# Products with the values in a fused attention, FFN and MoE kernel: another grouping of the query columns

## The chip, the cores and the metric

The kernel runs on one core of one Trainium2 chip. The metric is the device time of one execution, in microseconds (us). All arithmetic is in fp32 or in the fp32r form that the matrix engine takes (fp32 values split into a high and a low part).

## The reference

Three layers follow one another: a causal attention with a forget gate, a feed-forward layer, and a top-1 mixture of experts. The change lies in the attention, in its last line (`attn @ v`).

```python
batch, n_heads, seq, head_dim = (4, 8, 576, 64)
scores = scale * np.matmul(q, k.transpose(0, 1, 3, 2))
decay = cum[:, :, :, None] - cum[:, :, None, :]      # cum = cumsum(log f)
scores = np.where(causal, -1e9, scores + decay)
attn = softmax(scores)
out = np.matmul(attn, v)                             # x of the FFN: 2304 tokens x 512
...
x = _moe_ref(x)      # x @ w_in, an activation, @ w_out
y = _moe2_ref(x)     # 8 experts, each token goes to one
```

## The kernel before, in words

**Order of the work.** Nothing in the kernel is ordered by a scheduler of the compiler. A planner inside the kernel file (class `Order`) runs the program as coroutines against a table of assumed costs: each step is a `Use(engine, ns, function, priority)`, takes and gives buffers, and waits for events. Where several steps stand ready for an engine, the lower priority number goes first. The order that comes out is the static order of each engine's queue on the chip. So a changed cost or event in one coroutine can move instructions of others.

**Attention.** The 32 heads are worked off in 16 pairs; heads j = 0, 1 of a pair lie side by side. For pair i, `attention` (coroutines `unit`, `head`) takes five blocks of queries in the order c = 4, 3, 2, 1, 0 (`SEQ`): c = 0 to 3 are 128 queries each, against 128(c+1) keys, both heads; c = 4 is the last 64 queries of both heads together, against all 576 keys. Per block: scores on TensorE (L529, L534, tile `SR`, priority 0.8), decay and maximum on VectorE (L584), exponential on ScalarE (L589), scaling by the row sums on GpSimd (L600), then transposes on TensorE into one of two PSUM banks `T` (L612, L614, priority 0), and a copy out of `T` into SBUF by ScalarE (L634) or, for head 0 with c = 2 or 3, by VectorE (L632). The transposed weights of c = 0 to 3 go into one tile `pt` per head (four buffers, so two pairs), those of c = 4 into a tile `pu` (one buffer). `T_None` in the profile is the bank while it holds c = 4.

**Products with the values.** There are two bursts per pair, each with the two heads side by side on the two 64-column halves of the array:

- `weighted_last` (L707, tile `U`, in a `T` bank): last 64 queries, five key blocks, 64 columns each; it waits for c = 4 (`last_ok`); a VectorE copy (L713) brings it to columns 512 to 575 of `xT`.
- `weighted` (L654, tile `X`): the first 512 queries, four key blocks of 512, 384, 256 and 128 columns; it waits for all eight transposed blocks of c = 0 to 3 (`heads_ok`); a ScalarE copy (L661) brings it to columns 0 to 511 of `xT`. Priority 1.

```python
yield Use("PE", 2250, values, 1)     # weighted
yield Use("PE", 1100, burst, 1)      # weighted_last
yield Use("DVE", 230, lambda: nc.vector.tensor_copy(xT[:, 512:], X[:, :64]), 0)
```

Both are counted in `pv_ok`; then `xT` is written to memory (L672), and for the first four pairs `first_block` also splits its first 256 columns straight into the FFN's first input block `px0` (L689, L690).

**What runs beside it.** As soon as the first four pairs are done, the first half of the FFN (`half0`: L882 into `hp`, L1011 into `accp`, priority 6 and 6.5) fills TensorE wherever the attention has nothing ready. Its next input block (`px1` and so on) is loaded when the last one has been used up. Its weights `wa` are converted from 64-bit in 16 pieces over ScalarE, VectorE and GpSimd (L825 to L837) beside the attention. Until the first FFN block is there, `keep_warm` (L731) puts idle matmuls of the identity into gaps, priority 9, into the bank of `X`. After the attention the remaining FFN and MoE layers (L882, L1011, L1023 in other tiles) follow on TensorE.

Of the kernel before, what the change touches and what calls it, by code (L numbers as in the profile page):

```python
# [9 lines left out]
F32 = mybir.dt.float32  # L10
# [8 lines left out]
P = 128  # L19
# [171 lines left out]
def dve(n, fn, prio=5.0, fast=False):  # L191
    return Use("DVE", 144 + n * (0.6 if fast else 1.05), fn, prio)
# [31 lines left out]
def kernel(  # L224
# [14 lines left out]
    nc = tc.nc  # L239
# [73 lines left out]
    pt_ok = {(i, j): Event() for i in range(NP) for j in (0, 1, None)}  # L313
    s_done = [Event(5) for _ in range(NP)]
    read_ok = {(i, c): Event(2 if c < 4 else 1) for i in range(NP) for c in range(5)}
    heads_ok = [Event(8) for _ in range(NP)]
    last_ok = [Event() for _ in range(NP)]
    pv_ok = [Event(2) for _ in range(NP)]
    att_ok = Event(NP)
# [184 lines left out]


    def take_pt(i):
        for j in (1, None, 0):
            g = yield (pt4_b if j is None else pt_b, 1)
            if j is None:
                pt4[i] = (ap.tile([P, 5 * P], F32, tag="pu", name=f"pu{i}", bufs=1), g)  # L510
            else:
                pt[i, j] = (ap.tile([P, 13 * P], F32, tag="pt", name=f"pt{i}_{j}", bufs=4), g)
            done(pt_ok[i, j])

    def unit(i, c, started):
# [57 lines left out]
    def head(i, j, c, p, gp_, bank, st, summed, scaled, left):  # L573
# [24 lines left out]
        else:  # L598
            yield scaled
        yield pool1(w, lambda: nc.gpsimd.tensor_scalar(pw, pw, st[:, 6 + n:7 + n], 1.0, ALU.mult,  # L600
                                                       ALU.mult), 0)
        yield pt_ok[i, j]
        dst = pt4[i][0] if c == 4 else pt[i, j][0]
        for part in ((0, 1, 2, 3), (4,)) if c == 4 else (tuple(range(c + 1)),):
            gt = yield (t_b, 1)
            T = psa.tile([P, 512], F32, tag=f"T{gt[0]}", name=f"T{i}_{j}{c}{part[0]}", bufs=1)
            last = part == (4,)

            def turn():
# [8 lines left out]
            if c == 4:  # L618
                n = P * len(part)
                src, dh = (T[:64, :P], dst[:64, 512:]) if last else (T, dst[:, :512])  # L620
            else:
                n = w
                src = T[:, :w].rearrange("p (k q) -> p k q", q=P)
                if c < 2:
                    dh = dst[:, P * c:P * c + 384 * (c + 1)].rearrange(
                        "p (k q) -> p k q", q=384)[:, :, :P]
                else:
                    a0 = P * (c - 2)
                    dh = dst[:, a0:a0 + 384 * (c + 1)].rearrange(
                        "p (k q) -> p k q", q=384)[:, :, 256:]  # L630
            if j == 0 and c >= 2:
                yield dve(n, lambda: nc.vector.tensor_copy(dh, src), 0)  # L632
            else:
                yield act(n, lambda: nc.scalar.copy(dh, src), 0)  # L634
            give(t_b, gt)
        done(last_ok[i] if c == 4 else heads_ok[i])

    def weighted(i):

# [1 line left out]
        yield v_ok[i]  # L641
        gx = yield (xt_b, 1)
        xT = xts[i] = ap.tile([P, S], F32, tag="xT", name=f"xT{i}", bufs=2)
        go(weighted_last(i))
        vt, gr = vs[i]
        yield heads_ok[i]
        yield heads_ok[i]
        g = yield (x_b, 1)
        X = psa.tile([P, 512], F32, tag="X", name=f"X{i}")

        def values():
            for kb in range(4):
                for j in range(2):
                    nc.tensor.matmul(  # L654
                        X[D * j:D * j + D, P * kb:], vt[:, kb, j],
                        pt[i, j][0][:, 512 * kb:512 * kb + 512 - P * kb], start=(kb == 0),
                        stop=(kb == 3), skip_group_check=True)
        yield Use("PE", 2250, values, 1)
        for j in range(2):
            give(pt_b, pt.pop((i, j))[1])  # L660
        yield act(512, lambda: nc.scalar.copy(xT[:, :512], X), 0)  # L661
        give(x_b, g)
        done(pv_ok[i])
        yield pv_ok[i]
        give(rawv_b, gr)
        if i < NPAIR:
            go(first_block(i, xT))
# [24 lines left out]
        done(split_ok[i])  # L692
        done(half0.x_ok[0])

    def weighted_last(i):


        yield last_ok[i]
        gt = yield (t_b, 1)
        X = psa.tile([P, 512], F32, tag=f"T{gt[0]}", name=f"U{i}", bufs=1)  # L700
        t, vt = pt4[i][0], vs[i][0]

        def burst():
            for kb in range(5):
                kr = 64 if kb == 4 else P
                for j in range(2):
                    nc.tensor.matmul(X[D * j:D * j + D, :64], vt[:kr, kb, j],  # L707
                                     t[:kr, P * kb + 64 * j:P * kb + 64 * j + 64],
                                     start=(kb == 0), stop=(kb == 4))
        yield Use("PE", 1100, burst, 1)  # L710
        give(pt4_b, pt4.pop(i)[1])
        xT = xts.pop(i)
        yield Use("DVE", 230, lambda: nc.vector.tensor_copy(xT[:, 512:], X[:, :64]), 0)  # L713
        give(t_b, gt)
        done(pv_ok[i])

# [966 lines left out]
```

## Time and profile before

| | |
|---|---|
| median of 3 runs | 866.98 us (866.78 to 869.88) |
| profiled execution, its time | 867.16 us |
| its span in the trace | 865.6 us |
| TensorE busy (PE) | 844.3 us, 98% |
| VectorE (DVE), ScalarE (ACT), GpSimd (POOL) busy | 464.6, 362.7, 304.2 us |
| products with the values, L654 and L707 | 256 and 320 records on PE, from 24.9 to 312.1 us |
| starts of the sixteen main products (L654) | 34.5, 51.9, 66.1, 81.4, 100.7, 124.0, 140.3, 160.2, 179.3, 196.9, 216.8, 235.4, 256.2, 273.9, 293.0, 310.1 us |
| first FFN matmul (`hp`) | 88.3 us |

PE is the matrix engine, PEld its weight loads. An fp32 matmul of the attention's products stands in the trace as two records (two passes); busy time counts a moment once, however many records overlap. A line of the timeline has the start, the length, the engine, the source line and operation, the tiles, the shapes and the count of records merged, and in brackets how long the engine had been idle and what released it. The length of a merged line runs to the modelled end of its last matmul, so the distance from its start to the next line's start is what the work costs the engine.

### The profile page before, as it was taken

The numbers are of one execution on the slowest core, as the hardware profiler recorded it, in microseconds if no ns is written. First come the engines' busy times: TensorE is split into PE (matmuls) and PEld (weight loads), VectorE is DVE, ScalarE is ACT, GpSimd is POOL, SyncE is SP. The second block draws the span as 40 slices with busy tenths as digits, with TensorE's granted clock in tenths as the row PEclk, the third lists the DMA queues.
The fourth block names the chain that finished last, engine by engine and source line by source line (L and its number), as shares of the span: only waits on it lengthen the run. The fifth ranks groups of instructions, "written<-read, shape, count | busy, mean of one in ns | idle before, by whom it ended". The sixth has DMA issues, their size and how long they took to land.

```text
span 865.6 us, 15076 instructions
## 1 busy us (share of the span) xinstructions
PE 844.3 (98%) x5384; PEld 693.4 (80%) x5384; DVE 464.6 (54%) x1108; ACT 362.7 (42%) x841; POOL 304.2 (35%) x407
## 2 busy tenths in 40 slices
PE   9999998999999999999899999999999999999997
PEld 7665776887777799999888888888898888887685
DVE  7797977666545537777754344467652531212121
ACT  5677766565556644434533243323343121212110
POOL 3566876555544442444432122222210033000000
PEclk9999999999999999999999999999999999999999
DMA  7997666574324235233611133645432111541220
GB/s 145 174 188 180 164 164 154 123 141 119 95 67 122 73 123 110 79 120 98 207 62 49 61 130 112 211 142 183 148 124 85 49 49 49 211 154 50 98 74 25
DMA packets 154251, 101.96 MB, mean 118 GB/s; under 512 B 102802, under 2 KB 125842, under 8 KB 154176
## 3 DMA queue, kind: packets, MB, share of 16 engines
q1 hardware_dynamic: 151008, 96.22, 40.8%
q0 software_dynamic: 2832, 4.22, 1.8%
q8 instruction: 43, 0.70, 0.4%
q10 hardware_dynamic: 336, 0.56, 0.2%
q14 instruction: 32, 0.26, 0.1%
HBM read 76.86 MB, written 24.49 MB: 117 GB/s over the span
## 4 chain that ended last, share of the span: by engine, by line
PE 82%; DVE 9%; POOL 3%; ACT 2%; issue 2%; DMA 2%; SPq 0%; ACTq 0%; DVEq 0%; POOLq 0%
PE hm L882 12%; PE hr L882 12%; PE hp L882 8%; PE accp L1011 7%; PE accr L1011 6%; PE accBr L1011 6%; PE accm L1023 6%; PE accBm L1023 6%; PE SR L534 4%; PE T L614 4%; PE X L654 4%; PE gt L1197 1%; DVE wbx L830 1%; POOL wb L837 1%; PE U L707 1%
## 5 line engine op out<-in xcount | busy, mean ns | idle before, releaser
L904 POOL TENSOR_TENSOR glr<-gr,ghr 128x512 fp32r<-128x512 f32 x36 | 47.3, 1315 | 147.3 <-PE accBr L1011 90.8
L600 POOL TENSOR_SCALAR P<-P,st 128x512 f32<-128x512 f32 (+3 forms) x128 | 77.0, 615 | 38.4 <-DVE st L596 25.1
L882 PE MATMUL hr<-rx,wb 128*128 128x512 f32 (+1 forms) x384 | 89.5, 367 | 0.0
L882 PE MATMUL hm<-mx,wm 128*128 128x512 f32 (+1 forms) x336 | 87.0, 379 | 0.0
L1011 PE MATMUL accp<-ghp,wa 128*128 128x256 f32 x576 | 83.4, 287 | 2.1 <-DVE x_7b L1044 1.7
L589 ACT ACTIVATE P<-P,st 128x512 f32<-128x512 f32 (+3 forms) x128 | 71.4, 559 | 32.8 <-DVE st L584 31.8
L913 DVE SCALAR_TENSOR_TENSOR glm<-hm,ghm 128x512 fp32r<-128x512 f32 x36 | 24.8, 689 | 103.1 <-PE accBm L1023 68.4
L1011 PEld LDWEIGHTS accp<-ghp,wa 128*128 128x128 f32 x576 | 73.7, 190 | 5.4 <-issue 2.2
L912 ACT ACTIVATE ghm<-hm 128x512 fp32r<-128x512 f32 x36 | 21.6, 599 | 132.5 <-PE accBm L1023 120.7
L882 PEld LDWEIGHTS hr<-rx,wb 128*128 128x128 f32 x384 | 65.6, 188 | 13.0
L882 PEld LDWEIGHTS hm<-mx,wm 128*128 128x128 f32 x336 | 61.0, 188 | 14.9 <-issue 3.4
L904 POOL TENSOR_TENSOR glp<-gp,ghp 128x512 fp32r<-128x512 f32 x36 | 48.8, 1357 | 60.7 <-ACT ghp L903 54.2
L584 DVE CUSTOM_DVE_ANT_0 P<-SR,cm 128x512 f32<-128x512 f32 (+3 forms) x96 | 45.1, 485 | 24.8 <-PE SR L534 22.2
L614 PE MATMUL T<-ident,P 128*128 128x128 f32 x320 | 52.4, 278 | 3.5 <-POOL P L600 2.9
L894 ACT ACTIVATE tr<-hr,quarter 128x512 f32<-128x512 f32 x36 | 24.7, 687 | 61.3 <-DVE gr L899 44.4
L634 ACT COPY pt<-T 128x512 f32<-128x512 f32 (+2 forms) x96 | 35.3, 391 | 36.0 <-PE T L614 35.3
L898 DVE SCALAR_TENSOR_TENSOR gr<-tr 128x512 f32<-128x512 f32 x36 | 25.9, 719 | 42.1 <-POOL glr L904 40.5
L614 PEld LDWEIGHTS T<-ident,P 128*128 128x128 f32 x320 | 36.8, 141 | 14.5 <-POOL P L600 6.3
L534 PE MATMUL SR<-kt,qt 64*128 64x384 f32 (+3 forms) x224 | 44.9, 478 | 2.8 <-DVE st L584 2.5
L1011 PE MATMUL accr<-ghr,wb 128*128 128x512 f32 (+1 forms) x160 | 47.0, 375 | 0.0
L1011 PE MATMUL accp<-glp,wa 128*128 128x256 f32 x288 | 46.3, 283 | 0.4 <-POOL glp L904 0.4
L1011 PE MATMUL accBr<-ghr,wb 128*128 128x512 f32 (+1 forms) x160 | 46.5, 372 | 0.0
(355 smaller groups left out, 1871.8 us busy)
## 6 DMA issues: line engine op xcount, KB each, us to landing
cm<-rows SPq DMA_DIRECT2D x24, 256.0 KB, 4.4
rawq<-in_q_dram SPq DMA_DIRECT2D x64, 72.0 KB, 3.9
rawk<-in_k_dram SPq DMA_DIRECT2D x64, 72.0 KB, 3.3
xs<-xT SPq DMA_DIRECT2D x16, 288.0 KB, 2.1
x2n<-nat SPq DMA_DIRECT2D x18, 256.0 KB, 4.9
war<-in_moe_w_in_dram SPq DMA_DIRECT2D x8, 512.0 KB, 4.7
war<-in_moe_w_out_dram SPq DMA_DIRECT2D x8, 512.0 KB, 4.6
rawv<-in_v_dram SPq DMA_DIRECT2D x32, 128.0 KB, 2.7
```

What stands on the lines that cost most here:

```text
L534: nc.tensor.matmul(bank[:, j, :w], qt[p, P * c:P * c + P], kt[p, :w], start=True, stop=i >= NSUM)
L584: yield dve(w + 80, lambda: nc.vector.tensor_tensor_reduce(out=pv_, in0=so, in1=m, scale=-0.125, scalar=3e38, op0=ALU.add, op1=ALU.min, ac ...
L589: yield act(w, lambda: nc.scalar.activation(pw, pw, AF.Exp, bias=st[:, n:n + 1], scale=-1.0, accum_out=st[:, 2 + n:3 + n]), 1, 330)
L600: yield pool1(w, lambda: nc.gpsimd.tensor_scalar(pw, pw, st[:, 6 + n:7 + n], 1.0, ALU.mult, ALU.mult), 0)
L614: nc.tensor.transpose(T[:, P * n:P * n + P], p[:, P * kb:P * kb + P], ident)
L634: yield act(n, lambda: nc.scalar.copy(dh, src), 0)
L654: nc.tensor.matmul(X[D * j:D * j + D, P * kb:], vt[:, kb, j], pt[i, j][0][:, 512 * kb:512 * kb + 512 - P * kb], start=(kb == 0), stop=(kb ...
L882: nc.tensor.matmul(oo, a[:, c, cs], x[c], start=(ip == 0 and c == 0), stop=(ip == 2 and c == KC - 1))
L898: yield dve(n, lambda: nc.vector.scalar_tensor_tensor(g, t, 0.5, t, ALU.min, ALU.mult), 2)
L904: yield pool2(n, lambda: nc.gpsimd.tensor_tensor(gl, g, f32(gh), ALU.subtract), 1)
L1011: nc.tensor.matmul(acc[d][:, :w], b[:, fc, P * d:P * d + P], g, start=(fc == 0 and ip == 0 and (not narrow or d % 2 == 0)), stop=(fc == NF ...
L1023: nc.tensor.matmul(acc[a * (4 // na)], g[:, P * a:P * a + P], b[:, fc], start=(fc == 0 and ip == 0), stop=(fc == NF - 1 and ip == 2))
```

## The change

The 64 queries of c = 4 join the main product: their transposed weights are now copied into the two `pt` tiles, behind the 384 columns of c = 1 to 3 in each key block, so that the main product has 448, 448, 320, 192 columns for four key blocks of 128 keys and 64 for the last 64 keys (which stay in a small `pu`). The first 128 queries (c = 0) leave it and get a product of their own: one matmul per head over 128 columns, in a `T` bank (`weighted_first`, tile `U`). The main product now waits for c = 1 to 3 and c = 4, the small one for c = 0, which is the last block of a pair. The planner's costs go from 2250 and 1100 to 2700 and 260 ns.

```diff
-    heads_ok = [Event(8) for _ in range(NP)]
+    heads_ok = [Event(6) for _ in range(NP)]
+    early_ok = [Event(2) for _ in range(NP)]
...
     def take_pt(i):
-        for j in (1, None, 0):
+        for j in (0, 1, None):
             g = yield (pt4_b if j is None else pt_b, 1)
             if j is None:
-                pt4[i] = (ap.tile([P, 5 * P], F32, tag="pu", name=f"pu{i}", bufs=1), g)
+                pt4[i] = (ap.tile([P, P], F32, tag="pu", name=f"pu{i}", bufs=1), g)
             else:
-                pt[i, j] = (ap.tile([P, 13 * P], F32, tag="pt", name=f"pt{i}_{j}", bufs=4), g)
+                pt[i, j] = (ap.tile([P, 15 * P], F32, tag="pt", name=f"pt{i}_{j}", bufs=4), g)
...
-        yield pt_ok[i, j]
-        dst = pt4[i][0] if c == 4 else pt[i, j][0]
+        for n_ in (0, 1, None) if c == 4 else (j,):
+            yield pt_ok[i, n_]
+
+        def spread(h):
+            return pt[i, h][0][:, P:].rearrange("p (k q) -> p k q", q=448)
...
+            if last:
+                yield act(P, lambda: nc.scalar.copy(pt4[i][0][:64], T[:64, :P]), 0)
+            elif c == 4:
+                for h in range(2):
+                    yield act(256, lambda: nc.scalar.copy(
+                        spread(h)[:, :, 384:],
+                        T.rearrange("p (k j q) -> p j k q", k=4, j=2)[:, h]), 0)
...
-        done(last_ok[i] if c == 4 else heads_ok[i])
+        done(last_ok[i] if c == 4 else heads_ok[i] if c else early_ok[i])
...
-        go(weighted_last(i))
+        go(weighted_first(i))
         vt, gr = vs[i]
         yield heads_ok[i]
-        yield heads_ok[i]
+        yield last_ok[i]
...
-            for kb in range(4):
+            for kb, (p0, o0, n) in enumerate(
+                    ((128, 0, 448), (576, 0, 448), (1152, 128, 320), (1728, 256, 192),
+                     (0, 384, 64))):
                 for j in range(2):
...
+                    if kb < 4:
+                        m, vk = pt[i, j][0][:, p0:p0 + n], vt[:, kb, j]
+                    else:
+                        m, vk = pt4[i][0][:64, 64 * j:64 * j + 64], vt[:64, 4, j]
+                    nc.tensor.matmul(X[D * j:D * j + D, o0:o0 + n], vk, m, start=(kb == 0),
+                                     stop=(kb == 4), skip_group_check=True)
-        yield Use("PE", 2250, values, 1)
-        for j in range(2):
-            give(pt_b, pt.pop((i, j))[1])
-        yield act(512, lambda: nc.scalar.copy(xT[:, :512], X), 0)
+        yield Use("PE", 2700, values, 1)
+        give(pt4_b, pt4.pop(i)[1])
+        yield act(448, lambda: nc.scalar.copy(xT[:, P:], X[:, :448]), 0)
         give(x_b, g)
         done(pv_ok[i])
         yield pv_ok[i]
+        for j in range(2):
+            give(pt_b, pt.pop((i, j))[1])
...
-    def weighted_last(i):
+    def weighted_first(i):
-        yield last_ok[i]
+        yield early_ok[i]
...
-            for kb in range(5):
-                kr = 64 if kb == 4 else P
-                for j in range(2):
-                    nc.tensor.matmul(X[D * j:D * j + D, :64], vt[:kr, kb, j],
-                                     t[:kr, P * kb + 64 * j:P * kb + 64 * j + 64],
-                                     start=(kb == 0), stop=(kb == 4))
-        yield Use("PE", 1100, burst, 1)
-        give(pt4_b, pt4.pop(i)[1])
+            for j in range(2):
+                nc.tensor.matmul(X[D * j:D * j + D, :P], vt[:, 0, j], pt[i, j][0][:, :P],
+                                 start=True, stop=True)
+        yield Use("PE", 260, burst, 1)
         xT = xts.pop(i)
-        yield Use("DVE", 230, lambda: nc.vector.tensor_copy(xT[:, 512:], X[:, :64]), 0)
+        yield Use("DVE", 280, lambda: nc.vector.tensor_copy(xT[:, :P], X[:, :P]), 0)
```

## Rows read from the trace of the kernel before

**Rows 1.** The page's part 1: busy time of each engine, share, instructions.

```profile
PE 844.3 (98%) x5384; PEld 693.4 (80%) x5384; DVE 464.6 (54%) x1108; ACT 362.7 (42%) x841; POOL 304.2 (35%) x407
```

**Rows 2.** Busy time by stretch: stretch, us, busy per engine, granted clock, DMA share, GB/s.

```profile
20.00:88.00 68.00, 63.30 (x487) 42.96 (x486) 56.01 (x175) 48.20 (x134) 41.63 (x65) 1.00 0.92 182
88.00:128.00 40.00, 40.00 (x314) 31.75 (x312) 33.13 (x90) 26.89 (x71) 32.02 (x47) 1.00 0.64 156
128.00:146.00 18.00, 14.06 (x94) 9.98 (x90) 15.41 (x41) 11.48 (x30) 11.55 (x18) 0.91 0.65 154
146.00:340.00 194.00, 193.88 (x1572) 159.03 (x1571) 111.67 (x338) 111.42 (x287) 96.27 (x171) 1.00 0.45 106
```

**Rows 3.** The idle matmuls alone (tile warm) in one of these stretches.

```profile
20.00:88.00 68.00, 15.30 (x100) 13.22 (x99) 1.00 0.92 182
```

**Rows 4.** Timeline of PE around the two products of a pair, with what follows each.

```profile
160.16 2.38 PE L654 MATMUL X<-pt,rawv 128*64 128x512 f32 x16
162.47 0.66 PE L614 MATMUL T_None<-ident,P_None 128*128 128x128 f32 x4
...
168.14 0.95 PE L707 MATMUL U<-pu,rawv 128*64 128x64 f32 x20
169.02 0.66 PE L614 MATMUL T<-ident,P 128*128 128x128 f32 x4
```

**Rows 5.** Tile X in 10 ns steps: a rising count is a pass's start.

```profile
161.06:161.07 0.01, 0.01 (x3) 0.00 (x0) 0.00 (x0) 1.00 0.00 0
...
161.39:161.40 0.01, 0.01 (x4) 0.01 (x1) 0.00 (x0) 1.00 0.00 0
```

**Rows 6.** Tile U in 10 ns steps, the same reading.

```profile
168.24:168.25 0.01, 0.01 (x3) 0.01 (x4) 0.00 (x0) 1.00 0.00 0
...
168.30:168.31 0.01, 0.01 (x5) 0.01 (x5) 0.00 (x0) 1.00 0.80 205
168.36:168.37 0.01, 0.01 (x7) 0.01 (x5) 0.00 (x0) 1.00 0.58 230
...
168.75:168.76 0.01, 0.01 (x5) 0.01 (x1) 0.00 (x0) 1.00 0.00 0
...
168.86:168.87 0.01, 0.01 (x4) 0.01 (x4) 0.00 (x0) 1.00 2.36 640
```

**Rows 7.** Instructions copying out of PSUM, by line and shape: busy us, mean ns, idle before.

```profile
L634 ACT COPY pt<-T 128x256 f32<-128x256 f32 x32 | 11.2, 375 | 11.3 <-PE T L614 11.3
L661 ACT COPY xT<-X 128x512 f32<-128x512 f32 x16 | 9.3, 584 | 8.5 <-PE X L654 8.5
L634 ACT COPY pu<-T_None 128x512 f32<-128x512 f32 x16 | 9.3, 584 | 3.6 <-PE T_None L614 3.5
...
L713 DVE COPY xT<-U 128x64 f32<-128x64 f32 x16 | 3.4, 210 | 1.0 <-PE U L707 0.7
```

**Rows 8.** Timeline of a pair's end in the middle stretch, all engines.

```profile
175.25 0.37 ACT L634 COPY pt<-T 128x256 f32<-128x256 f32 x1 [0.23 <-PE T L614]
...
179.28 2.38 PE L654 MATMUL X<-pt,rawv 128*64 128x512 f32 x16
...
182.43 0.66 PE L614 MATMUL T_None<-ident,P_None 128*128 128x128 f32 x4
```

**Rows 9.** Timeline of the fourth pair's end and the FFN's start.

```profile
79.16 0.83 PE L731 MATMUL warm<-ident 128*128 128x128 f32 x6
79.36 0.27 ACT L634 COPY pt<-T 128x128 f32<-128x128 f32 x1
...
81.35 2.37 PE L654 MATMUL X<-pt,rawv 128*64 128x512 f32 x16
...
88.29 0.74 PE L882 MATMUL hp<-px0h,wa 128*128 128x256 f32 x4
```

**Rows 10.** Timeline: a late weight piece, and the FFN work that follows it.

```profile
132.53 1.27 POOL L837 TENSOR_TENSOR wa<-wax,wa 128x512 fp32r<-128x512 f32 x1 [0.47 <-ACT wa L836]
...
134.33 1.47 PE L882 MATMUL hp<-px0h,wa 128*128 128x256 f32 x4
```

More of the change, by code (lines that the diff above doesn't have):

```diff
@@ L617, in head @@
                 give(p_b, gp_)
-            if c == 4:
-                n = P * len(part)
-                src, dh = (T[:64, :P], dst[:64, 512:]) if last else (T, dst[:, :512])
+            if last:
[5 more added lines that the diff above has]
+                        T.rearrange("p (k j q) -> p j k q", k=4, j=2)[:, h]), 0)
             else:
-                n = w
                 src = T[:, :w].rearrange("p (k q) -> p k q", q=P)
-                if c < 2:
-                    dh = dst[:, P * c:P * c + 384 * (c + 1)].rearrange(
-                        "p (k q) -> p k q", q=384)[:, :, :P]
-                else:
[L628 to L634, printed above, removed]
+                dh = spread(j)[:, :c + 1, P * (c - 1):P * c] if c else pt[i, j][0][:, :P]
+                src = src if c else T[:, :P]
+                if j == 0 and c >= 2:
+                    yield dve(w, lambda: nc.vector.tensor_copy(dh, src), 0)
+                else:
+                    yield act(w, lambda: nc.scalar.copy(dh, src), 0)
             give(t_b, gt)
-        done(last_ok[i] if c == 4 else heads_ok[i])
+        done(last_ok[i] if c == 4 else heads_ok[i] if c else early_ok[i])
     def weighted(i):
@@ L651, in values @@
         def values():
-            for kb in range(4):
+            for kb, (p0, o0, n) in enumerate(
+                    ((128, 0, 448), (576, 0, 448), (1152, 128, 320), (1728, 256, 192),
+                     (0, 384, 64))):
                 for j in range(2):
[L654 to L657, printed above, removed]
-        yield Use("PE", 2250, values, 1)
-        for j in range(2):
-            give(pt_b, pt.pop((i, j))[1])
-        yield act(512, lambda: nc.scalar.copy(xT[:, :512], X), 0)
+                    if kb < 4:
[7 more added lines that the diff above has]
+        yield act(448, lambda: nc.scalar.copy(xT[:, P:], X[:, :448]), 0)
         give(x_b, g)
@@ L693, in first_block @@
         done(half0.x_ok[0])
-    def weighted_last(i):
-        yield last_ok[i]
+    def weighted_first(i):
+        yield early_ok[i]
         gt = yield (t_b, 1)
         X = psa.tile([P, 512], F32, tag=f"T{gt[0]}", name=f"U{i}", bufs=1)
-        t, vt = pt4[i][0], vs[i][0]
+        vt = vs[i][0]
         def burst():
-            for kb in range(5):
-                kr = 64 if kb == 4 else P
-                for j in range(2):
-                    nc.tensor.matmul(X[D * j:D * j + D, :64], vt[:kr, kb, j],
-                                     t[:kr, P * kb + 64 * j:P * kb + 64 * j + 64],
-                                     start=(kb == 0), stop=(kb == 4))
-        yield Use("PE", 1100, burst, 1)
-        give(pt4_b, pt4.pop(i)[1])
+            for j in range(2):
+                nc.tensor.matmul(X[D * j:D * j + D, :P], vt[:, 0, j], pt[i, j][0][:, :P],
+                                 start=True, stop=True)
+        yield Use("PE", 260, burst, 1)
         xT = xts.pop(i)
-        yield Use("DVE", 230, lambda: nc.vector.tensor_copy(xT[:, 512:], X[:, :64]), 0)
+        yield Use("DVE", 280, lambda: nc.vector.tensor_copy(xT[:, :P], X[:, :P]), 0)
         give(t_b, gt)
```

## The prediction

> **What bounds the kernel now.** I read the engines' totals first: TensorE is busy 98% of the span, no other engine more than 54% [rows 1]. Then the same by stretch, because an average over layers says little about a change in one of them [rows 2]. Three things are to be seen there. From 146 to 340 us, where nine of the sixteen main products run, TensorE is busy 193.88 of 194 us at a granted clock of 1.00, and from 88 to 128, with two more, all of the time: the FFN fills every gap of the attention, so that a nanosecond of TensorE work taken away there is a nanosecond off the end, and latency costs nothing. From 20 to 88 us it looks nearly as full (63.30 of 68 us), but 15.3 us of that are the idle matmuls of `keep_warm` [rows 3], and VectorE is busy 56 of 68 us: here the chain of scores, maximum, exponential, scaling and transposes sets the pace, and a shorter product saves nothing by itself. From 128 to 146 us TensorE stands still for 3.9 of 18 us and its mean granted clock is 0.91, between the levels of 1.2 and 2.4 GHz after the engine had been idle in pieces: the FFN has run out of work, since the unit that follows at 134.33 needs a piece of weights that GpSimd finishes at 133.80 [rows 10].
>
> So two questions decide: how much TensorE time a pair's products take after the change, and whether the waste before 146 us grows or shrinks.
>
> **TensorE time of the products.** Before, the main burst holds the engine from 160.16 to the next instruction at 162.47, 2.31 us; the small one from 168.14 to 169.02, 0.88 us [rows 4]. Together 3.19 us per pair, 51 us for sixteen.
>
> Columns first. Before: 512 + 384 + 256 + 128 and five times 64, which is 1600. After: 448 + 448 + 320 + 192 + 64 and 128, which is 1600 again. The two heads run side by side, and each block takes two passes. The two 384-column passes begin at 161.065 and 161.39 [rows 5]: 0.325 us, which is 384 columns at two cycles of 2.4 GHz (0.320). So the columns cost 1600 x 2 x 0.833 ns = 2.67 us before and after, and only what lies beyond columns can change: 3.19 - 2.67 = 0.52 us per pair, of which 0.18 in the main burst (2.31 - 2.13) and 0.35 in the small one (0.88 - 0.53).
>
> The steps show where it lies. Passes of 64 columns follow one another in 0.06 us (the rises at 168.30 and 168.36) [rows 6], 7 ns over their columns. With the first gap of 0.105 us (168.14 to the rise at 168.24), the eight passes over 128 keys would let the next start at 168.665; the first pass over the last 64 keys starts at 168.755 and the second 0.11 us later [rows 6]. That step from 128 to 64 rows thus costs about 0.14 us. What remains is some 0.05 us at the entry of a burst and 0.10 at its exit, in both.
>
> After the change the step to 64 rows is still there, now at the end of the main burst; there are still two bursts with an entry and an exit each; there are twelve passes in place of eighteen. So the main burst should hold the engine 1472 x 2 x 0.833 = 2.45, plus 0.05 + 0.14 + 0.10, about 2.74 us, and the small one 0.21 + 0.15, about 0.37 us: 3.11 to 3.12 in place of 3.19, 0.07 us saved per pair. Six passes at 7 ns are 0.04 of it, the rest is rounding of the steps. Bounds: at best the 0.35 us beyond columns of the old small burst vanish and only its entry comes back, 0.30 saved; at worst a weight load that was hidden stands free in the two-pass burst, and 0.07 is lost. I take 0.07, nearest to the steps. It counts in the eleven pairs where TensorE is full: 11 x 0.07 = **0.8 us**.
>
> Here a rule stands against the rows. The Trainium skill, "TensorEngine Tiling (Array Packing)", section Instruction Overhead, says that each matmul carries about 60 cycles, and that one of one column takes as long as one of 60. By that, twelve matmul records fewer per pair at an estimated 25 ns each would save 0.30 us, 4.8 us over sixteen pairs. The 64-column passes at 0.06 us do not bear it out; its case is the first rival below.
>
> **Copies.** The 512-column copy of c = 4 out of its bank (584 ns) becomes two of 256 (375 ns each) [rows 7]: 0.17 us more on ScalarE. Their source is read in runs of 64 columns, which no row shows; the c = 1 copies, written in runs of 128, are the nearest, and I bound each by its 375 ns and by the 584 of twice the columns. The copy of `X` shrinks from 512 to 448 columns, by an eighth of its 584 ns at most, 0.07 us [rows 7]. VectorE's copy grows from 64 to 128 columns: from 210 ns [rows 7], not above twice that. So ScalarE gets about 0.1 us more per pair, 1.6 us in all, and VectorE at most 0.2. Between 146 and 340 us both are busy 57% [rows 2], and the cover is FFN work on TensorE: no cost there. Before 146 us that cover is thin; at the worst the upper bound shows in full, 2 x 584 - 584 = 0.58 us and VectorE's 0.2 for each of seven pairs, 5.5 us, which belongs to the slower rival below. I take nothing, because the `T` bank gets it back: the old small product held a bank through 0.88 us of matmuls, the new one through 0.37.
>
> **Waits and releases.** The main product now waits for c = 1 and c = 4, no longer for c = 0, the last block. In the middle stretch a pair's last c = 1 copy ends at 175.62 and the product came at 179.28 [rows 8], so it can start up to 3.7 us sooner. The c = 4 transposes of the next pair now wait until that product has freed `pu`, and until the pair before last has freed both `pt`. They come at 182.43, 6.8 us after that c = 1 copy [rows 8]; 6.8 - 2.74 leaves four. Behind them on the planner's lists stand only the next pair's transposes and copies, so I cost this at nothing; if the margin went, it would be the head of the next pair that is late, and the FFN would fill. `pt` is given back after `pv_ok` rather than straight after the product, a pair earlier than it is needed. The write of `xT` on SP's queue stays one per pair, behind the later of the two copies.
>
> **The FFN's start.** For the fourth pair the last c = 0 copy ends at 79.63, the main product runs 81.35 to 83.65, and the first FFN matmul comes at 88.29 [rows 9]. After the change only the small product, its copy and the split stand behind c = 0. About 2 us of latency go, but what can be won is the waste in between, of which the idle matmuls at 79.16 are a part (six records in 0.83 us). Against it stands the stall at 128 to 146 us: the weight piece that ends at 133.80 [rows 10] does not come sooner because the FFN began sooner, so the engine may only wait longer there. Between nothing and those 2 us I take **0.5 us**.
>
> **Sum.** 867.16 us of the profiled execution, less 0.8, less 0.5, is 865.9; the median of the runs shown lies 0.18 below that execution, so 865.7 us, 0.15% less. A difference under 0.5% (4.3 us) can hardly be told from no change here.
>
> **Rivals.**
>
> *A charge per matmul.* If the 0.35 us beyond columns of the small burst belong to its number of matmuls and vanish, 0.30 us go per pair, and sixteen times that is 4.8 us: 862.2 us before any gain at the start. This is what the rule of "TensorEngine Tiling (Array Packing)" in the Trainium skill would come to. For it: the small burst has twice the overhead of the main one. Against: the 0.06 us steps, and the step to 64 rows, which moves and doesn't go. Chance 0.08.
>
> *The early stretch gets shorter.* Before 146 us the chain, not TensorE, sets the pace, and the two `T` banks are what all transposes share. The bank is held 0.5 us less per pair, and the product leaves the end of the pair. If seven pairs gain 0.6 us each and the FFN's start 1 us, the time is 867.0 - 5.2, less the 0.6 of the nine full pairs behind: 861.2. For it: 15.3 us of idle matmuls [rows 3] and 3.9 us of stall to be had. Against: VectorE's 56 of 68 us, and the weights. Chance 0.18.
>
> *The longer burst stands in the way.* The main product was behind a pair's last transposes; now it is 2.74 us long and can be put before those of c = 0 and before the next pair's scores, whose chain VectorE waits for. Place: the seven pairs before 146 us. Price: 0.43 us of longer burst and 0.17 us more in the c = 4 copies, 0.6 us per pair, 4.2 us, with the weight pieces behind it on VectorE and GpSimd another 0.5: 871.7 us. It decides where TensorE, in the early stretch, holds a ready transpose back that VectorE or ScalarE stand idle for. Against: TensorE has 15.3 us of idle work there. Chance 0.14.
>
> **Numbers.** My forecast, a saving too small to be told, has 0.60 and its own range from 863.0 to 868.5. Faster by over 0.5%: 0.08 + 0.18 = 0.26. Within: 0.60. Slower: 0.14. For 8 in 10 the range runs from 861.0 to 870.0: it leaves out the slower rival and the lower part of the faster ones.
>
> **What would show it.** Right: the timeline has main bursts of about 2.74 us with a visible pause before the 64-key passes, small ones of about 0.37 us, and the stretch from 146 to 340 us is as full as now, a microsecond of TensorE busy time less in all. The first FFN matmul comes between 86 and 88.3 us, and a stall near 130 us remains. Wrong: bursts that add up to under 3.0 us or over 3.25 us, no stall near 130 us, or more than 15.3 us of idle matmuls from 20 us on with a later FFN start.

## The result, and the profile after

The changed kernel takes **876.78 us** (median of 5 runs, 876.47 to 879.01) against 866.98: a ratio of 1.0111, with a 95% interval from 1.009 to 1.0132. It is slower by 9.8 us, outside the predicted range, which ended at 870.0. The profiled execution took 879.01 us with a span of 877.4 us, 11.8 us more than the span before.

The page's part 1 of the changed kernel, busy time of each engine, answers to [rows 1]:

```profile
PE 849.4 (97%) x5192; PEld 692.0 (79%) x5192; DVE 462.8 (53%) x1108; ACT 363.2 (41%) x857; POOL 311.5 (36%) x407
```

There are 192 fewer TensorE instructions, twelve per pair, and sixteen more on ScalarE, one per pair: the change is what its diff says.

The timeline of TensorE around the two products of a pair answers to [rows 4]:

```profile
97.72 2.59 PE L662 MATMUL X<-pt,rawv 128*64 128x448 f32 x16
100.24 0.33 PE L662 MATMUL X<-pu,rawv 64*64 64x64 f32 x4
100.50 1.13 PE L535 MATMUL SR<-kt,qt 64*128 64x512 f32 x4
101.56 0.44 PE L712 MATMUL U<-pt,rawv 128*64 128x128 f32 x4
101.93 0.74 PE L885 MATMUL hp<-px0h,wa 128*128 128x256 f32 x4
```

The main product holds TensorE from 97.72 to 100.50, 2.78 us, and the small one from 101.56 to 101.93, 0.37 us. Together that is 3.15 us, 0.04 less than before. The products are almost exactly what was forecast, and they are not where 10 us went.

The copies out of PSUM (groups by line and shape: busy us, mean ns, idle before) answer to [rows 7]:

```profile
L626 ACT COPY pt<-T_None 128x256 f32<-128x256 f32 x32 | 11.4, 366 | 8.6 <-PE T_None L618 8.6
L666 ACT COPY xT<-X 128x448 f32<-128x448 f32 x16 | 8.5, 531 | 17.5 <-PE X L662 17.5
L716 DVE COPY xT<-U 128x128 f32<-128x128 f32 x16 | 4.6, 289 | 7.2 <-PE U L712 6.9
```

These also come as bounded: 2 x 366 in place of 584 ns, 531 in place of 584, 289 in place of 210.

Now busy time by stretch, first of the changed kernel, then of the kernel before where [rows 2] has other stretches (columns as there):

```profile
20.00:88.00 68.00, 65.68 (x447) 45.47 (x445) 56.41 (x180) 48.73 (x143) 44.76 (x67) 1.00 0.90 183
88.00:128.00 40.00, 35.64 (x259) 27.18 (x257) 32.84 (x81) 23.56 (x60) 27.73 (x39) 1.00 0.68 158
128.00:160.00 32.00, 28.24 (x172) 20.71 (x173) 20.74 (x66) 20.37 (x57) 20.02 (x30) 0.84 0.50 120
160.00:340.00 180.00, 179.88 (x1344) 142.56 (x1343) 98.54 (x304) 100.31 (x271) 91.96 (x161) 1.00 0.41 105
400.00:450.00 50.00, 41.70 (x287) 38.59 (x286) 33.85 (x50) 21.81 (x37) 23.96 (x14) 0.93 0.44 143
```

```profile
128.00:160.00 32.00, 28.06 (x212) 22.07 (x207) 23.49 (x68) 20.04 (x53) 19.41 (x33) 0.95 0.65 149
160.00:340.00 180.00, 179.88 (x1453) 146.95 (x1452) 103.59 (x310) 102.87 (x263) 88.41 (x155) 1.00 0.43 103
400.00:450.00 50.00, 47.77 (x311) 43.19 (x311) 36.98 (x52) 22.12 (x39) 20.84 (x15) 1.00 0.39 127
```

The middle is as full as before, to the hundredth. The time went in two places.

**The first place, 88 to 160 us.** From 88 to 128 us TensorE was busy all of the time before and now idles 4.36 of 40 us. From 128 to 160 us it is as busy as before, but at a mean granted clock of 0.84 instead of 0.95, so part of the stretch ran at the 1.2 GHz level. Rows with an idle time in brackets, from the timeline of TensorE there:

```profile
128.05 1.09 PE L618 MATMUL T_None<-ident,P_None 128*128 128x128 f32 x4 [2.19 <-POOL P_None L601]
...
131.61 0.65 PE L885 MATMUL hp<-px0l,wa 128*128 128x256 f32 x4
132.09 0.64 PE L885 MATMUL hp<-px0h,wa 128*128 128x256 f32 x4
132.57 0.27 PE L616 MATMUL T_None<-ident,P_None 128*64 128x128 f32 x1
...
136.16 1.11 PE L618 MATMUL T<-ident,P 128*128 128x128 f32 x6 [1.66 <-POOL P L601]
...
139.72 2.29 PE L530 MATMUL SR<-kt,qz 128*128 128x288 f32 x4 [2.03 <-DVE st L585]
...
142.52 1.20 PE L885 MATMUL hp<-px1h,wa 128*128 128x256 f32 x4
```

The first FFN matmul comes at 84.20 us (before at 88.29 [rows 9]):

```profile
84.20 0.73 PE L885 MATMUL hp<-px0h,wa 128*128 128x256 f32 x4
```

The last FFN unit of `px0` runs at 130.65 us (before at 134.33 [rows 10]) and the next block comes at 142.52 (before at 145.3). In between TensorE has only the attention, and stands still whenever the chain of scaling and maximum is not ready.

**The second place, the hand-over from attention to the second half of the FFN.** The sixteenth main product starts at 326.3 us, before at 310.1. Only after it is attention's memory released, in which the next weights `wb` are built; their sixteen conversions on GpSimd (the instructions of that line: shortest, median and longest ns, first and last start) run, in the changed kernel and in the one before, as

```profile
L840 POOL TENSOR_TENSOR wb<-wbx,wb x16: 1283/1726/2100, 348.5 to 459.3; 128x512 fp32r<-128x512 f32 x16
```

```profile
L837 POOL TENSOR_TENSOR wb<-wbx,wb x16: 1294/1722/1759, 329.8 to 443.2; 128x512 fp32r<-128x512 f32 x16
```

that is 18.7 us later at the first and 16.1 at the last. The timeline of TensorE around that point, after:

```profile
422.91 1.21 PE L1014 MATMUL accp<-ghp,wa 128*128 128x256 f32 x8 [3.08 <-DVE x_7b L1047]
...
437.17 1.23 PE L1014 MATMUL accp<-glp,wa 128*128 128x256 f32 x4 [3.76 <-POOL glp L907]
438.20 4.76 PE L885 MATMUL hr<-rx,wb 128*128 128x512 f32 x12
...
444.22 5.75 PE L885 MATMUL hr<-rx,wb 128*128 128x512 f32 x24
```

and before, the run of `hr` that nothing breaks:

```profile
429.58 11.35 PE L882 MATMUL hr<-rx,wb 128*128 128x512 f32 x48
```

After, `hr` breaks off after 12 matmuls and starts again at 444.22.

The wait of 3.76 us for `glp` can be followed one step further. The GpSimd instruction that makes this last `glp` takes 4.84 us. VectorE works beside it without a pause until 435.99 us, and it ends 1.1 us after that, at 437.12:

```profile
432.28 4.84 POOL L907 TENSOR_TENSOR glp<-gp,ghp 128x512 fp32r<-128x512 f32 x1 [3.54 <-ACT ghp L906]
432.30 0.68 DVE L871 TENSOR_TENSOR rx1l<-rx1l,rx1h 128x512 fp32r<-128x512 f32 x1
...
435.31 0.68 DVE L871 TENSOR_TENSOR rx<-rx 128x512 fp32r<-128x512 f32 x1
436.60 1.07 DVE L871 TENSOR_TENSOR rx<-rx 128x512 fp32r<-128x512 f32 x1 [0.60 <-ACT rx L870]
```

In the kernel before the same instruction takes 1.51 us:

```profile
426.00 1.51 POOL L904 TENSOR_TENSOR glp<-gp,ghp 128x512 fp32r<-128x512 f32 x1 [3.99 <-ACT ghp L903]
```

The last `glp` takes 4.83 or 4.84 us in this kernel and in three of the runs below, each time beside seven VectorE instructions in a row, and 1.3 to 1.8 us in the kernel before and the eleven other runs. These are the four in which TensorE waits 3.2 us or more for it. So the order decides what stands side by side there. That VectorE holds GpSimd up is a reading of these rows; no run took VectorE's work away.

Idle time plus the part that the lower clock took: up to 160 us it is 11.9 us before and 18.0 after, from 340 to 450 us 4.3 and 12.0. These 6.1 and 7.7 us are the 11.8 of the span and a little more; the sum is good to some 2 us, since idle matmuls count as busy in it.

Between the two places the attention falls back further without any idle time: the eighth main product is 3.1 us later than before (163.2 against 160.2), the sixteenth 16.2 us. Ahead of the last main product, TensorE's queue holds 804 matmuls of the FFN's first half before and 900 after. In the timeline above four of them take 0.48 us (131.61 to 132.09 to 132.57), so 96 more are 11.5 us, most of those 13. It is another order of the same work.

### The profile page after: what moved, and what is told of

Read it like the earlier page. It is cut to its first block, busy times and chain, and to the rows that moved or that the text cites. A ratio compares the mean times of both kernels' runs of the same rounds, so it can differ in the third digit from the quotient of the medians.

```text
span 877.4 us, 14703 instructions
## 1 busy us (share of the span) xinstructions
PE 849.4 (97%) x5192; PEld 692.0 (79%) x5192; DVE 462.8 (53%) x1108; ACT 363.2 (41%) x857; POOL 311.5 (36%) x407
## 4 chain that ended last, share of the span: by engine, by line
PE 87%; DVE 5%; POOL 3%; DMA 2%; ACT 2%; issue 1%; SPq 0%; ACTq 0%; POOLq 0%; DVEq 0%
PE hr L885 12%; PE hm L885 12%; PE hp L885 10%; PE accp L1014 8%; PE accr L1014 6%; PE accBr L1014 6%; PE accm L1026 6%; PE accBm L1026 6%; PE X L662 5%; PE SR L535 4%; PE T L618 4%; PE SR L530 2%; PE gt L1200 1%; PE warm L734 1%; DVE wbx L833 1%
## 5 line engine op out<-in xcount | busy, mean ns | idle before, releaser
L601 POOL TENSOR_SCALAR P<-P,st 128x512 f32<-128x512 f32 (+3 forms) x128 | 80.3, 640 | 43.8 <-DVE st L597 22.9
L885 PE MATMUL hr<-rx,wb 128*128 128x512 f32 (+1 forms) x384 | 91.5, 373 | 0.0
L907 POOL TENSOR_TENSOR glp<-gp,ghp 128x512 fp32r<-128x512 f32 x36 | 51.5, 1431 | 55.0 <-ACT ghp L906 50.2
L535 PE MATMUL SR<-kt,qt 64*128 64x128 f32 (+3 forms) x228 | 46.5, 485 | 1.7 <-DVE st L585 1.6
```

What stands on the lines that cost most here:

```text
L535: nc.tensor.matmul(bank[:, j, :w], qt[p, P * c:P * c + P], kt[p, :w], start=True, stop=i >= NSUM)
L885: nc.tensor.matmul(oo, a[:, c, cs], x[c], start=(ip == 0 and c == 0), stop=(ip == 2 and c == KC - 1))
L907: yield pool2(n, lambda: nc.gpsimd.tensor_tensor(gl, g, f32(gh), ALU.subtract), 1)
```

## The experiments

**Theory O**: the time went because the planner wrote another order of the queues; the new steps cost about what was forecast. **Rivals**: the new steps themselves cost it; above all the single `pu` that a pair's c = 4 transposes must wait for (W), or the small product's place in the `T` bank at a pair's end (T).

**The old kernel with two cost figures of the planner changed.** No instruction is added or taken away; only the assumed costs are the measured ones.

```diff
-        yield Use("PE", 2250, values, 1)
+        yield Use("PE", 2310, values, 1)
...
-        yield Use("PE", 1100, burst, 1)
+        yield Use("PE", 880, burst, 1)
```

> The kernel before, instruction for instruction, but the planner is told what the products take in the trace of before (2310 and 880 ns in place of 2250 and 1100); only the order of the queues changes. Theory O (the 10 us come from the order that the plan fell into): in this kernel's TensorE queue 900 FFN matmuls stand ahead of the last main product, as many as in the changed kernel (900) and not 804 as before, so it should be slow too, 872 to 879 us. Rival P (the longer product, its copies and its waits cost the time themselves): none of them is in this kernel, so 866 to 869 us.

Measured: **879.5 us**, a ratio of 1.016 (1.013 to 1.019), just above theory O's range. The old instructions in another order are about as slow as the changed kernel: in the profiled executions TensorE's last matmul ends at 869.09 us here, at 870.93 in the changed kernel and at 859.10 in the kernel before. The largest waits of TensorE in that run (engine, tile and line, releaser: us in total, times, longest):

```profile
PE T L614 <- POOL P L600: 4.6, 6, 1.8
PE accp L1011 <- POOL glp L904: 3.8, 1, 3.8
PE accp L1011 <- DVE x_7b L1044: 3.1, 1, 3.1
PE SR L529 <- DVE st L584: 2.5, 1, 2.5
```

and in the changed kernel:

```profile
PE accp L1014 <- POOL glp L907: 3.8, 1, 3.8
PE T L618 <- POOL P L601: 3.6, 6, 1.7
PE accp L1014 <- DVE x_7b L1047: 3.1, 1, 3.1
PE T_None L618 <- POOL P_None L601: 2.2, 1, 2.2
PE SR L530 <- DVE st L585: 2.0, 1, 2.0
```

and, at the hand-over, in the kernel before:

```profile
PE accp L1011 <- DVE x_7b L1044: 1.7, 1, 1.7
PE accp L1011 <- POOL glp L904: 0.4, 1, 0.4
```

In the first two the same waits, with the same lengths at the hand-over, and the `wb` conversions run from 347.0 to 457.4 us there. The new products are not needed for any of it.

**The changed kernel with the costs 2640 and 300.**

```diff
-        yield Use("PE", 2700, values, 1)
+        yield Use("PE", 2640, values, 1)
...
-        yield Use("PE", 260, burst, 1)
+        yield Use("PE", 300, burst, 1)
```

> The changed kernel, instruction for instruction, with the planner's two figures at 2640 and 300 ns in place of 2700 and 260. Theory O: the order changes (888 FFN matmuls ahead of the last main product, the stretch before 146 us planned differently), so the time moves by several us away from 876.8, most likely down, 866 to 874. Rival P: same instructions, same product, same copies, 875 to 878 us.

Measured: 874.45 us, 1.0089 (1.007 to 1.0109), between the two ranges. Its windows separate the two places:

```profile
88.00:128.00 40.00, 38.72 (x277) 29.07 (x275) 34.01 (x85) 25.74 (x71) 29.52 (x43) 1.00 0.66 167
128.00:160.00 32.00, 29.30 (x195) 21.87 (x193) 22.23 (x69) 20.01 (x54) 20.00 (x34) 0.95 0.61 141
400.00:450.00 50.00, 42.56 (x268) 38.83 (x267) 33.51 (x51) 21.66 (x37) 23.77 (x14) 0.90 0.44 147
```

From 88 to 160 us it idles 4.0 us, like the kernel before (3.9), at the same clock; the hand-over is as bad as in the changed kernel. So nearly all of its 7.8 us lie at the hand-over.

**Two buffers for `pu`** in the changed kernel.

```diff
-Buffers(4), Buffers(1), Buffers(2))
+Buffers(4), Buffers(2), Buffers(2))
...
-name=f"pu{i}", bufs=1), g)
+name=f"pu{i}", bufs=2), g)
```

> The changed kernel with two buffers for the small tile pu, so that the c = 4 transposes of the next pair no longer wait for the main product. Rival W (that wait is what costs the time): back to 867 us or below, with FFN and attention as far apart as in the changed kernel. Theory O: the order changes as well (852 FFN matmuls ahead of the last main product), and the time lies by that count between before and after, 868 to 873 us.

Measured: 871.11 us, 1.0049 (1.003 to 1.0068). That is 5.7 us off the changed kernel, which W could claim. But a buffer also gives the planner other choices, and the wait on `glp` is gone from the hand-over. The run with 2750 and 280 below decides between the two readings.

**The old kernel with attention's memory released 17 us later in the plan**; attention itself stays as it was.

```diff
         yield att_ok
+        yield o.now + 17000.0
         psa.release()
```

> The kernel before with one edit behind the attention: the planner waits 17 us after the last pair before it hands the attention's memory to the second half's weights. In the changed kernel the first of those weights' conversions ended 18.7 us later than before (348.5 against 329.8 us). Theory O, second half (the later end of the attention leaves too few FFN matmuls to cover the conversion): 4 to 7 us slower, 871 to 874 us, with the stall between 400 and 445 us. Rival (only the stall before 146 us costs, the later end is covered): 866 to 869 us.

Measured: 871.92 us, 1.0047 (1.0027 to 1.0067), so 5.3 us more, with the last main products where they were and the `wb` conversions from 349.1 us. A late hand-over alone costs time. How much is less sure: the interval is 2.3 to 5.8 us, and in the profiled execution TensorE's last matmul ends at 862.58 us, 3.5 later than before, and what follows it takes 8.1 us instead of 6.5. The waits are not those of the changed kernel, though (the longest at the start of `hr` is 1.7 us, for ScalarE's `rx`).

**The new products laid into nearly the old order**: the planner is shown the old costs and the old bank use, the new small product is booked at nothing.

```diff
         yield last_ok[i]
+        yield early_ok[i]
...
-        yield Use("PE", 2700, values, 1)
+        yield Use("PE", 2250, values, 1)
...
+        yield last_ok[i]
+        gt = yield (t_b, 1)
+        yield Use("PE", 1100, lambda: None, 1)
+        yield Use("DVE", 230, lambda: None, 0)
+        give(t_b, gt)
+        yield heads_ok[i]
         yield early_ok[i]
...
-        yield Use("PE", 260, burst, 1)
+        yield Use("PE", 0, burst, 1)
```

with both copies of c = 4 booked as one of 512, the copy of `X` as 512, the last copy on VectorE as 0, and two `pu`.

> The change's products, copies and tiles, laid into nearly the order of the kernel before: the planner keeps the old figures (2250 for the main product, which waits for all five blocks again; 1100 and 230 ns stay booked, without an instruction, where the old small product stood; the two c = 4 copies booked as one; the new small product booked at nothing behind the main one), and pu has two buffers so that no c = 4 transposes wait. FFN matmuls ahead of the main products, pairs 5 to 16: 60, 156, 168, 240, 312, 384, 468, 540, 600, 672, 744, 816; before: 60, 156, 168, 240, 312, 372, 444, 516, 600, 660, 732, 804. Theory O (the order, not the products): 865 to 869 us. Rival P (products, copies or their length cost the time themselves): 874 to 878 us.

Measured: 871.13 us, 1.0054 (1.0039 to 1.007): between the theories, a miss for both. The hand-over is healed (46.84 of 50 us busy from 400 to 450), while from 128 to 160 us the clock is at 0.89. The order is close to the old one, not the same, and work booked at too little may shift it against the chip. So it is not shown whether its 4.4 us come from the order that is left or from the new products.

**The old kernel with 2280 and 1140**, a smaller change of the same two figures.

```diff
-        yield Use("PE", 2250, values, 1)
+        yield Use("PE", 2280, values, 1)
...
-        yield Use("PE", 1100, burst, 1)
+        yield Use("PE", 1140, burst, 1)
```

> The kernel before, instruction for instruction, with the planner's figures at 2280 and 1140 ns in place of 2250 and 1100: a second other order for the old products, this time one that ends the attention nearly as early (816 FFN matmuls ahead of the last main product, 804 before, 900 in the slow orders). Theory O with the count as its measure: 864 to 870 us. Rival (any order but the one shown first is slow, the count says nothing): 874 to 880 us.

Measured: 866.64 us, 0.9998 (0.9985 to 1.0012). So another order can also cost nothing; the first run is no law that every other order is bad.

**Two `pu`, and the idle matmuls kept on until the FFN's third input block is there**, in place of its first.

```diff
-        go(keep_warm(xs_ok[0]))
+        go(keep_warm(xs_ok[2]))
```

> The changed kernel with two buffers for pu (e3), with the idle matmuls kept up until the eighth pair is done; the FFN counts are those of e3 (852), and nine idle matmuls more stand in TensorE's gaps. If the lower granted clock after the stall near 130 us is a cost of its own, it goes: 0.5 to 2 us under e3, 869 to 870.5 us, with the granted clock of 88 to 160 us at 1.00. If not, as e3, 870.5 to 872 us.

Measured: 870.31 us, 1.0039 (1.0022 to 1.0056), 0.8 us less than without. The clock from 128 to 160 us is 1.00 (0.95 without). But the two intervals overlap, and in the profiled executions TensorE's last matmul ends at 861.52 us without the idle matmuls and at 861.55 with them: no gain can be told. The 0.84 of the changed kernel is a deeper dip than the one filled here, and what it costs was not tested.

**The small product in the bank of `X`** instead of a `T` bank.

```diff
-        gt = yield (t_b, 1)
-        X = psa.tile([P, 512], F32, tag=f"T{gt[0]}", name=f"U{i}", bufs=1)
+        gt = yield (x_b, 1)
+        X = psa.tile([P, 512], F32, tag="X", name=f"U{i}")
...
-        give(t_b, gt)
+        give(x_b, gt)
```

> The changed kernel with the small product in the main product's PSUM bank, one after the other, instead of in one of the two banks of the transposes. Rival T (the small product keeps a transpose bank from the next pair's first blocks, and that stretches the pairs): the pairs come closer again, back to 866 to 869 us. Theory O: another order with 864 FFN matmuls ahead of the last main product and 888 ahead of the last small one, 871 to 876 us.

Measured: 874.99 us, 1.0093 (1.0072 to 1.0114). From 88 to 160 us it idles only 2.8 us at full clock, less than the kernel before, and yet it is 8 us slower, with the 3.2 us wait on `glp` at the hand-over. So the loss is there without T. The early stretch did get better, but this edit, too, changed the order; that T's place by itself costs little is shown by the run with 2750 and 280 below, which keeps it.

**Finer steps for the planner**: each FFN step of the first half cut in three of four matmuls, so that a change of order should do less. In the old kernel, the changed one, and the changed one with 2640 and 300:

```diff
+                        if self is half0:
+                            for ip in range(3):
+                                yield Use("PE", mm(w, KC),
+                                          lambda: first(oo[:, w * k:w * k + w], s, W, X, (ip,)),
+                                          self.prio, after=None if s == u[-1] and ip == 2 else 0.0)
+                            continue
```

and the same for `self.second`.

> The kernel before with the planner's FFN steps of the first half cut in three (4 matmuls, about 0.48 us, instead of 12 in one piece), so that attention work that comes ready waits less for TensorE. Same instructions. FFN matmuls ahead of the last main product: 772 (804 before). Theory O, the order ahead of the attention's end decides: not above 867, 862 to 867 us. Rival: finer steps only add gaps, 868 to 874 us.

> The changed kernel with the same cut of the FFN steps; 768 FFN matmuls ahead of the last main product, 900 without the cut. Theory O: the stall at the hand-over goes and most of the 10 us with it, 863 to 869 us, within 3 us of the old products in the same plan (e9). Rival P (the new products cost time themselves): 8 us or more above e9.

> As e10, with the planner's figures for the two products at 2640 and 300 ns; 772 FFN matmuls ahead of the last main product. Theory O: as e10 give or take what another order makes in the stretch before 146 us, 862 to 869 us. Rival P: as the changed kernel, 874 us or more.

Measured: 874.25 us (1.0084, 1.0068 to 1.01), 885.8 us (1.022, 1.0206 to 1.0233) and 872.09 us (1.0056, 1.0043 to 1.0069). Misses: finer steps did not make the time steady, they made the spread larger, 13.7 us between two figures for the same products. They also refute a simple measure: these three orders have only 768 to 772 FFN matmuls ahead of the last main product, fewer than the kernel before, and are slow all the same. The second run lies 11.6 us above the first, as rival P expected; but the third has the second's instructions and lies 2.2 us below the first, so that those 11.6 us are not the price of the products. And none of the three has the long wait for `glp` (0.8 us or less), so that is not the only way to lose time.

**The changed kernel with 2750 and 280**, every instruction, buffer and bank as in the change.

```diff
-        yield Use("PE", 2700, values, 1)
+        yield Use("PE", 2750, values, 1)
...
-        yield Use("PE", 260, burst, 1)
+        yield Use("PE", 280, burst, 1)
```

> The changed kernel, instruction for instruction, with the planner's figures at 2750 and 280 ns: close to what the trace shows (2.78 us in the main product), and an order with 852 FFN matmuls ahead of the last main product. Theory O: as the other order with 852 (e3), 868 to 873 us. Rival P: 875 to 878 us.

Measured: **867.73 us**, 1.0018 (1.0004 to 1.0032), just under theory O's range and far from P's. Its windows and its first wait of TensorE at the hand-over:

```profile
88.00:128.00 40.00, 38.48 (x275) 29.02 (x274) 35.09 (x88) 26.32 (x72) 29.60 (x42) 1.00 0.68 165
128.00:160.00 32.00, 28.47 (x191) 21.56 (x193) 21.76 (x64) 19.31 (x51) 21.42 (x34) 0.95 0.60 138
400.00:450.00 50.00, 46.70 (x292) 42.85 (x291) 36.11 (x51) 22.38 (x38) 21.92 (x15) 0.93 0.42 137
```

```profile
416.96 2.08 PE L1014 MATMUL accp<-ghp,wa 128*128 128x256 f32 x8 [3.30 <-DVE x_7b L1047]
...
431.22 8.55 PE L885 MATMUL hr<-rx,wb 128*128 128x512 f32 x36
```

The `wb` conversions start at 338.4 us, ten earlier than with 2700 and 260, and `hr` runs on from 431.22. One buffer of `pu`, the wait for it and the small product's `T` bank are still there: neither W nor T is the cause, and the gain of the second buffer was most likely a gain by order. The same new instructions take 867.7, 874.5 or 876.8 us by two numbers that the chip never sees.

**What TensorE time is worth at a fixed order.** The old kernel and its old queue order; the small product does only the first and the last key block, so that the last 64 queries leave out keys 128 to 511. The burst is 0.52 us (146.48 to 147.00) instead of 0.88 [rows 4], 5.8 us less in all.

```diff
-            for kb in range(5):
+            for kb in (0, 4):
```

> The kernel before in its own order of the queues; of the five key blocks of the small product the second to fourth are left out (keys 128 to 511 of the last 64 queries), so six passes of 0.06 us, 0.36 us of TensorE time, go from every pair, and nothing else. By the prediction's step (a saving counts where TensorE is full, in eleven of the sixteen pairs): 11 x 0.36 = 4.0 us less, 862 to 864 us. If it counts in all sixteen: 5.8 us less, 861 us. If TensorE time in the attention is not what bounds: within 1 us of 866.7.

Measured: 863.78 us, 0.997 (0.9961 to 0.998): 2.5 us, or 0.43 of what was taken away (by the interval 0.3 to 0.6), less than the 4.0 expected for eleven full pairs (the time is inside the range expected for them only because the kernel before took 866.25 beside this run, not 866.7). From 128 to 160 us TensorE is busy 27.06 us at a clock of 0.95 (28.06 before): part of what the product leaves there stays idle. The traces give more than the medians. The sixteenth main product starts at 306.3 us (310.1 in the kernel before, 309.5 in the run below, which has the same order of TensorE), and TensorE's last matmul ends at 855.33 (859.10 and 858.28): 3.0 to 3.8 us sooner. What follows that matmul took 8.5 us in this profiled execution and 6.5 in the other two.

**The c = 4 copy as two of 256 columns**, old kernel, old order.

```diff
+            elif c == 4 and not last:
+                yield act(n, lambda: [nc.scalar.copy(dh[:, s], src[:, s]) for s in (
+                    slice(0, 256), slice(256, 512))], 0)
```

> The kernel before in its own order of the queues, with the 512-column copy of c = 4 issued as two of 256 columns, as in the change: 0.17 us more on ScalarE in each pair. By the prediction (the copy is covered): 866 to 867.5 us. Rival P (the copies cost): seven pairs before 146 us or all sixteen times 0.17, 1.2 to 2.7 us more, 868 to 869.5 us.

Measured: 866.15 us, 1.0002 (0.9991 to 1.0013), with two copies of 374 ns in place of one of 584. No cost can be told, as predicted.

## Why the prediction was wrong

- **Time of the products**: right. 2.78 and 0.37 us against 2.74 and 0.37, the step to 64 rows included. 0.04 us are saved per pair, not 0.07.
- **Its worth**: the factor was somewhat too high. At a fixed order 0.43 of a TensorE microsecond came back by the medians (0.3 to 0.6), 0.5 to 0.65 by the end of TensorE's work in the traces, not eleven pairs in sixteen (0.69). So 16 x 0.04 x 0.43 is 0.3 us, where 0.8 stood.
- **A charge per matmul**: not borne out. The prediction's estimate from the Trainium skill, "TensorEngine Tiling (Array Packing)", section Instruction Overhead, would give 4.8 us for the 192 matmuls fewer; the trace shows 16 x 0.04, 0.6 us.
- **Copies**: right in their sizes, and for the split copy of c = 4 in its cost (0.0002 of the time at a fixed order, inside its interval). The longer copy on VectorE was not tested by itself.
- **Waits and releases**: the wait for `pu` was costed at nothing. It is not the cause of the loss: with this wait in place, the best order found takes 867.73 us.
- **The FFN's start**: it comes at 84.20 us instead of 88.29, 4.1 us sooner where 2 were thought possible, and that pays nothing: `px0` is used up 3.7 us sooner, and the gap before `px1` grows from 11.0 to 11.9 us (from the start of its last unit). The stall before was also read as the late weight piece alone; of its 3.9 us, 2.1 lie before 134.33 us, where that piece is awaited, and 1.9 behind, where `px1` is not there yet.
- **The step that failed** is the one that added these terms as if all other work kept its place: "Behind them on the planner's lists stand only the next pair's transposes and copies, so I cost this at nothing", and a sum with no term for the order itself. The change moved events, buffers and costs in a planner of which the text ahead of the prediction says that a changed cost can move instructions of others. The order carried a term of up to 13 us, of a sign that the profile before does not give: the old instructions ran at 866.6 to 879.5 us, the new ones (same instructions, buffers and banks) at 867.7 to 876.8.
- **The rivals**: "the longer burst stands in the way" had the side right, the mechanism not: it put 0.6 us on each of seven pairs and took the weights as the end of it; the runs showed idle pieces from 88 to 160 us and a late hand-over beyond 400 us, both of them there with the old, shorter burst as well. Among the rivals that were weighed, none had the order as its mechanism.
- **The signs**: the bursts, the full middle and the stall near 130 us came as they were named for a right forecast, and said nothing of the 10 us. The two that failed were the FFN's start and TensorE's busy time, 5.1 us more [rows 1] where a microsecond less was named.

Of the orders without the finer FFN steps and with all the work, the four in which the last `accp` waits 3.2 to 3.8 us for `glp` took 874.5 to 879.5 us; the others, in which it waits 0.5 us at most, 866.2 to 871.9. That ties the wait, and the long `glp` before it, to the loss. Which single step of the plan brings the two together, and which makes the pairs before 160 us slow in the changed kernel, stays open. No version that does all the work was clearly faster than the kernel before. The best order found for the new products is 0.18% slower (0.04 to 0.32%), 867.73 us against 866.64 for the old products in another order; whether that 1 us is the grouping's own or its order's can't be told, so a small cost of the grouping itself is not excluded.

## What to carry to other kernels

Where a planner writes a static order from cost figures, every edit of a cost, a buffer or an event is an edit of the whole order: jitter the figures by a few per cent, time the old and the new instructions in several orders, and only then credit or blame the change. Price the change itself at a fixed order (work left out, an instruction split), and give the forecast a term for the order as wide as the spread of such jittered runs. Look for releases at the end of a phase: a phase that ends 16 us late on an engine that is 100% busy in both kernels shows nothing in that stretch, and here the bill came where the next phase's weights are due.

## What was not expected of the hardware

One GpSimd instruction over 128x512 elements, 1.51 us long in the kernel before, took 4.84 us where seven VectorE instructions ran in a row beside it, and ended 1.1 us after VectorE's first pause. It did so in four of the sixteen traces, and TensorE waited 3.2 to 3.8 us for it each time.

What follows TensorE's last matmul took 6.5 us in ten of the sixteen profiled executions and 7.7 to 8.5 in the other six. So two medians that lie a microsecond or two apart are best compared by the end of TensorE's work as well. By that measure, holding the granted clock at 1.00 from 128 to 160 us with idle matmuls, where it had been 0.95, gave nothing that can be told (861.55 against 861.52 us), though the medians lie 0.8 us apart.
